# Storing the last 26 rows of a spectrum as cells of both parts, and regrouping the rows of the product that reads them

## The chip, the cores and the metric

The kernel runs on one core of one Trainium2 chip. TensorE (PE) multiplies matrices and writes to the PSUM banks, VectorE (DVE), ScalarE (ACT) and GpSimd (POOL) work on PSUM or SBUF, and SyncE (SP) issues nearly all DMAs, which 16 DMA engines carry out. The metric is the time of one execution on the device in microseconds. Three runs of the kernel before gave 803.3, 807.4 and 810.25 us, median 807.4 us. The profile is of one more execution, which took 805.76 us; the span from its first to its last instruction is 803.7 us.

## The reference

```python
def _attn_ref(x, h):                      # x (8, 5696, 128), h (5696, 128)
    B, S, D = x.shape
    L = 2 * S
    Yf = np.fft.rfft(x, n=L, axis=1) * np.fft.rfft(h, n=L, axis=0)[None]
    return np.fft.irfft(Yf, n=L, axis=1)[:, :S, :]

def _moe_ref(x, phi, w1, w2):             # x (45568, 128), phi (128, 32), 8 experts, F = 1024
    logits = x @ phi
    d = softmax(logits, over all 45568 tokens)
    slot_input = (d.T @ x).reshape(8, 4, 128)
    slot_out = relu(slot_input[e] @ w1[e]) @ w2[e]     # per expert e, 32 slots in all
    return softmax(logits, over the 32 slots) @ slot_out
```

A long causal convolution of eight sequences with one filter per channel is followed by a soft mixture of experts on the 45568 tokens that come out. Everything is float32.

## The kernel before

The convolution is a two-step Fourier transform of size 90 x 64 written as matrix products. Stage A (`low`, `high`, `fold`; lines 208 to 252) multiplies the input with the table `s1`. Stage B does, for each of 90 frequencies k (64 "main" ones and 26 more), a small transform forward (`stage_b1`, line 287), the product with the filter's spectrum on DVE (lines 306 and 313), and a small transform backward (`stage_b2`, line 328, result `bz`, copied by ACT into `zst`, line 333). Between the stages the data is turned round through DRAM: `fst` goes out to `fl` and `fh` and comes back as `gt`, and `zst` goes out to `zm` (the 64 main frequencies) and `zr` (the other 26) and comes back as `zc` and `zx`. In the last batches further buffers `zd` and `zy` are used.

Stage C works on 32 tiles of tokens, T = 0 to 31, four for each of the eight sequences. `stage_c1` (called `product` in the written order) is the last product of the transform. For each T it makes four PSUM banks `ps[o, c]`, with o for the cosine or sine half of z and c for its real or imaginary part. Each bank is [128, 512]: the upper and the lower 64 partitions hold two fold halves h_ = 0 and 1, of which 45 rows each carry results, and the 512 columns are 4 rows n of 128 channels. The main product (line 419) sums over 64 frequencies: the rows of SBUF are (o, k), so a matmul uses 64 rows and 64 columns of the PE array. The product that this change is about (line 424) adds the other 26 frequencies: the rows of `zx` are (o, c, k), 32 for each of the four pairs (o, c), of which 26 are used. Eight matmuls of 26 rows by 64 columns do it, one for each pair (o, c) and each half h_: rows by (o, c), columns by h_.

After the product ACT copies `ps[0, 1]` (line 427, tile `y`) and `ps[1, 0]` (line 428, tile `om`) to SBUF, and DVE forms sums and differences with `ps[0, 0]` and `ps[1, 1]` (lines 411 and 412). `sums` finishes them on POOL, in the tail of the kernel partly on DVE (line 437). Then come transposes (line 447), logits (456), exponentials, and the dispatch product (546). After all tiles come the experts (lines 801 to 836) and the output product (883).

All instructions are recorded in an order that is written out by hand: the strings of words in the calls of `run` (lines 648 to 725 and 842 to 853). Each word calls one stage for one tile, each engine executes its share in that order, and semaphores order the engines among each other. DMAs of results are collected in `pending` and issued by SP at the word `flush`; loads are issued where `loadf`, `loadx`, `loadz`, `loadr` or `load` stand. The pool of PSUM banks for stages A and C has four members until line 726 and eight afterwards.

The store of the last 26 rows is in `stage_b2`, lines 348 to 352: for each half o two DMAs, one for the real and one for the imaginary part, each reading 64 partitions and moving runs of 128 numbers (512 bytes). The load is `load_rest`, line 392: runs of 4 KB for each partition, 8 KB where two tiles come at once. The row order in z is set by `back` (line 54), a permutation of the columns of the backward table `vt`.

Of the kernel before, what the change touches and what calls it, by code (L numbers as in the profile page):

```python
# [12 lines left out]
F32 = mybir.dt.float32  # L13
# [6 lines left out]
def transform_tables(S, N1, N2, CH, LOW, MAIN):  # L20

    N, R1, HALF, P = N1 * N2, S // N2, N2 // 2, 2 * N2  # L30
    k1 = np.arange(N1)
    alpha = np.pi * (k1 + 0.5) / N1
    m1 = np.arange(R1) - (N1 - 1) / 2
    a1 = np.outer(m1, alpha)
    part = np.stack([np.cos(a1), -np.sin(a1), -np.cos(a1)], 1)
    s1 = np.zeros((P, 3, N2 + HALF))
    for p, r in ((slice(0, P, 2), slice(0, N2)), (slice(P - 4 * (R1 - N2) + 1, P, 4), slice(N2, R1))):
        s1[p, :, 0:LOW] = part[r, :, 0:LOW]
        s1[p, :, N2:N2 + N1 - LOW] = part[r, :, LOW:]
    a0 = np.outer(alpha, np.arange(N1 // 2) + 0.5)  # L40
    part = np.stack([np.cos(a0), -np.sin(a0), -np.cos(a0)], 1)
    NP = N1 // 2
    im = np.zeros((2, MAIN, 2, N2))
    ir = np.zeros((2, 2, HALF, N2))
    for o in range(2):
        for c in range(2):
            im[o, :, c, 0:NP] = part[0:MAIN, o + c]
            ir[o, c, 0:N1 - MAIN, 0:NP] = part[MAIN:, o + c]
    k2 = np.arange(N2)
    omega = np.pi * (k1[:, None] + 2 * N1 * k2[None] + 0.5) / N  # L50
    m2 = np.arange(HALF) - (N2 - 1) / 2
    a2 = m2[None, :, None] * omega[:, None, :]
    w = np.concatenate([np.cos(a2), np.sin(a2)], 1)
    back = np.arange(N2).reshape(2, HALF).T.reshape(-1)
    NU = (NP + 1) // 2
    turn = (N1 - 1) / 2 * alpha[:, None] + (N2 - 1) / 2 * omega
    wq = np.zeros((2, N2, NP, N2))
    vq = np.zeros((2, N2, NU, 2, N2))
    tn = np.zeros((2, N2, 2, (NU + 1) // 2, 2, 2))
    rows = np.arange(N2).reshape(2, HALF // CH, CH)  # L60
    near = rows.reshape(2, -1, 2, CH).transpose(3, 2, 0, 1).reshape(-1)
    far = rows.reshape(2, -1, 2, 2, CH).transpose(4, 2, 3, 0, 1).reshape(-1)
    for a in range(2):
        wq[a] = w[a::2].transpose(1, 0, 2)
        wq[a] = np.concatenate([wq[a][near, 0:LOW // 2], wq[a][far, LOW // 2:]], 1)
        for q in range(NP):
            vq[q % 2, :, q // 2, a] = w[2 * q + a][back].T
            tn[q % 2, :, 0, q // 4, a, q // 2 % 2] = np.cos(turn[2 * q + a]) / N
            tn[q % 2, :, 1, q // 4, a, q // 2 % 2] = np.sin(turn[2 * q + a]) / N
    im, ir, wq, vq, tn = [t.reshape(P, *t.shape[k:]) for t, k in  # L70
                          ((im, 2), (ir, 3), (wq, 2), (vq, 2), (tn, 2))]
    return [np.ascontiguousarray(t, dtype=np.float32) for t in (s1, im, ir, wq, vq, tn)]
# [3 lines left out]
def kernel(  # L76
# [24 lines left out]
    nc = tc.nc  # L101
    P = 128
    B, S, D = x.shape
# [4 lines left out]
    N1, N2 = 90, 64  # L108
    R1, HALF, NP = S // N2, N2 // 2, N1 // 2
# [19 lines left out]
    fh = [nc.dram_tensor(f"fh_{g}", (NJ // 4, 2, CH, 2, 2, 2, HALF // 2, 2 * D), F32, kind="Internal").ap()  # L129
          for g in range(B + 1)]  # L130
    zm = [nc.dram_tensor(f"zm_{b}", (2, MAIN, HALF, 2, D), F32, kind="Internal").ap() for b in range(B)]
    zr = [nc.dram_tensor(f"zr_{b}", (2, 2, HALF, HALF, D), F32, kind="Internal").ap() for b in range(2)]
    cd = nc.dram_tensor("c_t", (P, B * NQ, Q, 2, MH), F32, kind="Internal").ap()

    const = ctx.enter_context(tc.tile_pool(name="const", bufs=1))
# [3 lines left out]
    nc.gpsimd.memset(one[:, :], 1.0)  # L139
    phi = const.tile([D, NSL], F32, name="phi")  # L140
    im = const.tile([P, 2, HP], F32, name="im")
    ir = const.tile([P, HP], F32, name="ir")
    acc = const.tile([P, D + 1], F32, name="acc")
    NT = B * NQ
    TR = HP + MH
# [171 lines left out]
    def stage_b2(u):  # L317
        g, w, us = parts(u)
        if g == 0:
            return  # L320
        m = len(us)
        y_ = prods.pop(u)
        bz = bps.tile([P, 2, 2, 2 * D], F32, name="bz", tag=("bt", "bz")[u % 2])
        for o, (i, n) in enumerate(us):
            for q in range(n):
                r = slice(q * HP, (q + 1) * HP)
                for a in range(2):
                    nc.tensor.matmul(bz[a * HP:(a + 1) * HP, q, o, :], vt[r, i, a, :],  # L328
                                     y_[r, a * m + o, :, :].rearrange("p c d -> p (c d)"),
                                     start=True, stop=True)  # L330
        n = us[0][1]
        e_ = w % 4
        nc.scalar.activation(zst[:, e_, 0:m, 0:n, :].rearrange("p o q x -> p q o x"),  # L333
                             bz[:, 0:n, 0:m, :], AF.Copy)
        if w % 2 == 0:
            return
        k = 4 * e_ + m * n
        sv = zst[:, :, :, :, :].rearrange("p u o q x -> p (u o q) x")
        q0 = 4 * e_ - 4
        k0 = 8 * (w - 1)  # L340
        for o in range(2):
            if k0 < MAIN:
                pending.append(partial(
                    nc.sync.dma_start,
                    out=zm[g - 1][o, k0:k0 + 16].rearrange("(q a) r c d -> (a r) q (c d)", a=2),
                    in_=sv[o::2, q0:k, :]))
                continue
            for c in range(2):
                pending.append(partial(
                    nc.sync.dma_start,  # L350
                    out=zr[g % 2][o, c, k0 - MAIN:k0 - MAIN + 2 * (k - q0)].rearrange("(q a) r d -> (a r) q d", a=2),
                    in_=sv[o::2, q0:k, c * D:(c + 1) * D]))

    zs, ys, Ls, ds = {}, {}, {}, {}
    ybufs = [ypool.tile([P, Q * CH, D + 1], F32, name=f"y{i}") for i in range(2)]
    zring = [ypool.tile([P, 2, CH, 2, D], F32, name="zc")]
    rests, rest = [ypool.tile([P, 2, 2, CH, D], F32, name="zx")], {}
    lt = ypool.tile([P, CH, 2, HP], F32, name="lt")
    dt = ypool.tile([P, CH, 2, HP], F32, name="dt")
    om, op = [ypool.tile([P, CH, D], F32, name=n) for n in ("om", "op")]  # L360
# [8 lines left out]
    def load_main(T):  # L369
        if T >= NT:  # L370
            return
        b, j = divmod(T, NQ)
        t_ = zring.pop(0)
        zring.append(t_)
        zs[T] = t_
        n = 2 * CH
        nc.sync.dma_start(
            out=t_[:, :, :, :, :].rearrange("p h n c d -> p (h n c d)"),
            in_=zm[b].rearrange("o k r c d -> (o k) r (c d)")[:, j * n:(j + 1) * n].rearrange(
                "p r x -> p (r x)"))  # L380

    def load_rest(T):
        if T >= NT:
            return
        b, j = divmod(T, NQ)
        m = 1 if j < 2 else 2
        if j % 2 == 0:
            t_ = rests.pop(0)
            rests.append(t_)
            rest[T] = rest[T + 1] = t_  # L390
        n = 2 * CH
        nc.sync.dma_start(
            out=rest[T][:, j % 2:j % 2 + m, :, :, :].rearrange("p v h n d -> p (v h n d)"),
            in_=zr[(b + 1) % 2].rearrange("o c k r d -> (o c k) r d")[:, j * n:(j + m) * n].rearrange(
                "p r x -> p (r x)"))

    def load_pair(T):
        load_main(T)
# [2 lines left out]
    def stage_c1(T, between=lambda: None):  # L401
# [13 lines left out]
        for c in (1, 0):  # L415
            for h_ in range(2):
                for o in range(2):
                    r = slice(o * HP, (o + 1) * HP)
                    nc.tensor.matmul(ps[o, c][h_ * HP:(h_ + 1) * HP, :], im[r, c, :],  # L419
                                     zt[r, h_, :, c, :], start=True, stop=False)  # L420
        for h_ in range(2):
            for (o, c), p in ps.items():
                r = slice((2 * o + c) * HALF, (2 * o + c) * HALF + N1 - MAIN)
                nc.tensor.matmul(p[h_ * HP:(h_ + 1) * HP, :], ir[r, :], zx[r, h_, :, :],  # L424
                                 start=False, stop=True)
        ps = {k: p[:, :].rearrange("p (n d) -> p n d", d=D) for k, p in ps.items()}
        nc.scalar.activation(part(0, 0), ps[0, 1], AF.Copy)  # L427
        nc.scalar.activation(om[:, :, :], ps[1, 0], AF.Copy)
# [191 lines left out]
    nc.scalar.dma_start(out=phi[:, :], in_=moe_phi)  # L620
    nc.scalar.dma_start(out=turn[:, :, :, :, :], in_=t_turn)
    nc.scalar.dma_start(out=im[:, :, :], in_=t_im)
    nc.scalar.dma_start(out=ir[:, :], in_=t_ir)
    for i in range(8):
        nc.scalar.dma_start(
            out=zr[i // 4][i // 2 % 2, i % 2, N1 - MAIN:].rearrange("k (j r) d -> (k j) (r d)", r=2 * CH),
            in_=rests[0][0:4 * (HALF - N1 + MAIN), 0, :, :, :].rearrange("p h n d -> p (h n d)"))
    held = {}

    def load_w1(e_):  # L630
# [96 lines left out]
    rings.append(mid.enter_context(tc.tile_pool(name="ps2", bufs=4, space=PSUM)))  # L727
    last = work.enter_context(tc.tile_pool(name="last", bufs=1))
    tail["last"] = last
    zring.insert(0, last.tile([P, 2, CH, 2, D], F32, name="zd"))  # L730
    rests.insert(0, last.tile([P, 2, 2, CH, D], F32, name="zy"))
    tail["cT"] = last.tile([P, B, R1, 2 * NJ], F32, name="cT")
    second = inner.enter_context(tc.tile_pool(name="second", bufs=1, side="right"))
    w2s = second.tile([P, E, NFC, D], F32, name="w2s")
# [41 lines left out]
    def expert_in():  # L776
# [14 lines left out]
        nc.vector.tensor_copy(out=own, in_=p[:, 0:NSL].rearrange("p (e s) -> p e s", s=SPE))  # L791
    EG = E // Q
    FH = 512
    hid, hidT = [z_[:, :, :, :, :].rearrange("p h n c d -> p (h n c d)").rearrange(
        "p (g k c) -> p g k c", g=EG, k=NFC) for z_ in zring[::-1]]

    def layer_1(g):
# [138 lines left out]
```

## Time and profile before

| what | value |
|---|---|
| median of three runs (lowest to highest) | 807.4 us (803.3 to 810.25) |
| profiled execution: its time, its span | 805.76 us, 803.7 us |
| PE, DVE, ACT, POOL busy | 712.9, 629.3, 429.3, 410.4 us |
| DMA | 164779 packets, 282.50 MB, mean 352 GB/s |
| main product, line 419 | 512 records of MATMUL (32 tiles x 16) |
| product of the last rows, line 424 | 512 records of MATMUL (32 tiles x 16) |
| stores of `zr` | 32 DMAs of 256 KB and 32 of 160 KB |
| mean granted clock of TensorE | 0.951 |

How to read it: busy times are sums over the whole span, and a matmul's record runs until its modelled end, so overlapping matmuls make PE busy without telling how much it does. Each float32 matmul of the program leaves two MATMUL records and two weight loads: it is done in two passes. The slices and windows tell where in the span an engine is busy, and the chain of work that ended last tells which work set the end.

### The profile page before, as it was taken

The page shows a single profiled execution, that of the slowest core. Times are in us where ns is not written, and L with a number is a line of the kernel's source. Part 1 is how long each engine was busy: PE and PEld are TensorE (multiplying, and loading weights), DVE is VectorE, ACT ScalarE, POOL GpSimd, SP SyncE. Part 2 cuts the span into 40 slices and gives each one's busy share as a digit, 9 for nine tenths or more (in the row PEclk, how much of TensorE's full clock was granted, in tenths as well). Part 3 has the DMA queues.
Part 4 walks back from the last instruction along what each step waited for, and adds up shares of the span by engine and source line. Part 5 has one row for each costly group of instructions (what it writes and reads, how often), then busy time and mean ns, then how long its engine had stood idle before and what let it go on. Part 6 is the DMA issues. An engine that isn't in the chain of part 4 may idle for free.

```text
span 803.7 us, 21826 instructions
## 1 busy us (share of the span) xinstructions
PE 712.9 (89%) x8884; PEld 360.5 (45%) x8884; DVE 629.3 (78%) x895; ACT 429.3 (53%) x868; POOL 410.4 (51%) x368
## 2 busy tenths in 40 slices
PE   5768789779999999999999999999998887888882
PEld 1122233324544444554455455444444444356782
DVE  1019988648989999998999999999989996795552
ACT  2334245335666665666666566666565455474441
POOL 5545443425556666656666655566434533686000
PEclk9889999979999999999999999999999998999865
DMA  8999999999999999999999999999999899843998
GB/s 274 357 308 405 332 391 388 330 361 388 389 351 379 383 388 344 397 393 380 361 394 394 355 386 389 399 355 357 374 309 342 282 363 317 317 179 129 385 401 337
DMA packets 164779, 282.50 MB, mean 352 GB/s; under 512 B 9448, under 2 KB 128872, under 8 KB 158440
## 3 DMA queue, kind: packets, MB, share of 16 engines
q1 hardware_dynamic: 163672, 280.01, 96.1%
q8 instruction: 71, 1.16, 0.5%
q10 hardware_dynamic: 1008, 1.10, 0.4%
q14 instruction: 28, 0.23, 0.1%
HBM read 148.54 MB, written 132.53 MB: 350 GB/s over the span
## 4 chain that ended last, share of the span: by engine, by line
PE 62%; DVE 15%; DMA 14%; ACT 4%; issue 2%; POOL 1%; SPq 1%; ACTq 0%; DVEq 0%; POOLq 0%
PE bank L240 18%; PE bt L287 10%; PE bz L328 8%; PE bank L419 7%; DMA out_dram<-o 4%; PE bank L424 4%; PE bank L447 4%; DMA fl<-fst 4%; DVE yf L306 3%; DVE bt L306 3%; PE bank L456 3%; PE bank L546 2%; DVE yf L313 2%; PE bank L570 2%; DMA gt<-fh 2%
## 5 line engine op out<-in xcount | busy, mean ns | idle before, releaser
L216 POOL TENSOR_TENSOR x<-xc 128x512 f32<-128x512 f32 x144 | 179.1, 1276 | 81.5 <-PE bank L240 53.5
L240 PE MATMUL bank<-x,s 128*32 128x512 f32 x1728 | 207.1, 608 | 14.0 <-POOL x L216 8.1
L242 ACT ACTIVATE fst<-bank 128x512 f32<-128x512 f32 x216 | 125.6, 595 | 84.5 <-PE bank L240 63.3
L287 PE MATMUL bt<-gt,wt 64*64 64x256 f32 x1620 | 117.6, 399 | 26.2 <-DMA gt<-fl 9.7
L333 ACT ACTIVATE zst<-bz 128x1024 f32<-128x1024 f32 x96 | 93.0, 968 | 80.6 <-PE bz L328 74.3
L437 POOL TENSOR_TENSOR y<-y,op 128x512 f32<-128x512 f32 x64 | 78.3, 1223 | 105.2 <-DVE op L411 102.7
L306 DVE TENSOR_TENSOR yf<-bt,Hi 128x1024 f32<-128x1024 f32 x96 | 112.4, 1171 | 16.2 <-PE bt L287 16.1
L313 DVE TENSOR_TENSOR yf<-bt,yf 128x512 f32<-128x512 f32 x192 | 119.3, 663 | 3.3
L306 DVE TENSOR_TENSOR bt<-bt,Hr 128x1024 f32<-128x1024 f32 x96 | 113.0, 1177 | 0.0
L240 PEld LDWEIGHTS bank<-x,s 128*32 128x32 f32 x1728 | 52.2, 111 | 131.8 <-issue 91.8
L328 PE MATMUL bz<-yf,vt 64*64 64x256 f32 x1440 | 100.6, 387 | 4.6 <-DVE yf L313 4.2
L287 PEld LDWEIGHTS bt<-gt,wt 64*64 64x64 f32 x1620 | 54.9, 135 | 87.9 <-issue 35.6
L533 POOL TENSOR_TENSOR L<-L,rs 128x512 f32<-128x512 f32 x32 | 33.6, 1051 | 109.3 <-DVE rs L528 89.5
L328 PEld LDWEIGHTS bz<-yf,vt 64*64 64x64 f32 x1440 | 55.7, 136 | 39.8 <-DVE yf L313 11.8
L437 POOL TENSOR_TENSOR y<-y,om 128x512 f32<-128x512 f32 x54 | 64.1, 1187 | 2.1
L427 ACT ACTIVATE y<-bank 128x512 f32<-128x512 f32 x32 | 19.1, 597 | 81.6 <-PE bank L424 81.6
L447 PE MATMUL bank<-ident,y 109*128 109x109 f32 x512 | 59.4, 261 | 3.1 <-DVE y L437 1.0
L419 PE MATMUL bank<-zc,im 64*64 64x512 f32 x480 | 60.3, 600 | 0.0
L447 PEld LDWEIGHTS bank<-ident,y 109*128 109x128 f32 x512 | 49.7, 141 | 12.7 <-issue 7.9
L306 DVE TENSOR_TENSOR yf<-bt,turn 128x1024 f32<-128x1024 f32 (+1 forms) x12 | 14.0, 1170 | 52.4 <-PE bt L287 52.4
L449 ACT ACTIVATE yt<-bank 128x360 f32<-128x360 f32 x128 | 52.6, 475 | 3.7 <-PE bank L447 3.5
L883 PE MATMUL op<-so,cT 32*128 32x128 f32 x704 | 43.6, 357 | 6.5 <-ACT o L891 6.0
(99 smaller groups left out, 854.9 us busy)
## 6 DMA issues: line engine op xcount, KB each, us to landing
fl<-fst SPq DMA_DIRECT2D x72, 512.0 KB, 7.7
gt<-fl SPq DMA_DIRECT2D x72, 512.0 KB, 7.2
zm<-zst SPq DMA_DIRECT2D x64, 512.0 KB, 9.3
zc<-zm SPq DMA_DIRECT2D x30, 1024.0 KB, 9.1
fh<-fst SPq DMA_DIRECT2D x36, 512.0 KB, 6.6
xc<-in_x_dram SPq DMA_DIRECT2D x32, 512.0 KB, 8.8
out_dram<-o SPq DMA_DIRECT2D x16, 1024.0 KB, 11.2
gt<-fh SPq DMA_DIRECT2D x27, 512.0 KB, 8.2
```

The lines of the kernel that those rows point to most:

```text
L216: nc.gpsimd.tensor_tensor(out=y_[:, o, :, :], in0=near, in1=far, op=AL.subtract if o else AL.add)
L240: nc.tensor.matmul(p[i * m:(i + 1) * m, :], s1[:, q + o, cols], columns(c_, o), start=True, stop=True)
L242: nc.scalar.activation(st[:, :, q, :], p[:, :].rearrange("p (n d) -> p n d", d=D), AF.Copy)
L287: nc.tensor.matmul(bt[q * HP:(q + 1) * HP, a, o, :], wt[r, 2 * i + q, :], t_[r, 2 * o + q, :, :].rearrange("p c d -> p (c d)"), start=True ...
L306: nc.vector.tensor_tensor(out=p_, in0=pv, in1=h_, op=AL.mult)
L313: nc.vector.tensor_tensor(out=y_[r, 0:k, c, :], in0=pv[:, :, c, :], in1=y_[r, 0:k, c, :], op=op_)
L328: nc.tensor.matmul(bz[a * HP:(a + 1) * HP, q, o, :], vt[r, i, a, :], y_[r, a * m + o, :, :].rearrange("p c d -> p (c d)"), start=True, sto ...
L333: nc.scalar.activation(zst[:, e_, 0:m, 0:n, :].rearrange("p o q x -> p q o x"), bz[:, 0:n, 0:m, :], AF.Copy)
L419: nc.tensor.matmul(ps[o, c][h_ * HP:(h_ + 1) * HP, :], im[r, c, :], zt[r, h_, :, c, :], start=True, stop=False)
L437: eng.tensor_tensor(out=part_, in0=part(v, 0), in1=o_[:, :, :], op=sign)
L447: nc.tensor.transpose(p[:, i * TR:(i + 1) * TR], ys[T][0:TR, k * CH + i, 0:D], ident[0:TR, 0:TR])
L449: nc.scalar.activation(yt[:, k * CH:(k + 1) * CH, :, :], of_tokens(p), AF.Copy)
```

## The change

The last rows of z are stored as cells that hold both parts, real and imaginary, one behind the other. `zr` becomes (o, h, k, m, c, d): the fold half h moves to the outside, the part c to the inside. A store reads 32 partitions (every fourth) and moves runs of 256 numbers (1 KB); there are still four stores for each group of frequencies. The rows of `zx` are then (o, h, k), and its columns (m, c, d). So the matmuls of the last rows are grouped by (o, h) on the row side: the pair (o, h) picks both the rows and the column half, and the part c picks a slice of the moving data and a table in `ir`. They are issued by part, first for the banks `ps[0, 1]` and `ps[1, 0]`, then for the other two. Their stationary operand has 45 columns in place of 64, since the 19 zero columns are gone. For both products to see the same rows, the order of the backward columns (`back`) changes, and with it the layout of `zc`: (n, h, c, d) in place of (h, n, c, d). The written order of the stages is the same.

```diff
-    ir = np.zeros((2, 2, HALF, N2))
+    ir = np.zeros((2, 2, HALF, 2, NP))
...
-            ir[o, c, 0:N1 - MAIN, 0:NP] = part[MAIN:, o + c]
+            ir[o, :, 0:N1 - MAIN, c] = part[MAIN:, o + c]
...
-    back = np.arange(N2).reshape(2, HALF).T.reshape(-1)
+    back = np.arange(N2).reshape(2, -1, 2, CH).transpose(1, 3, 2, 0).reshape(-1)
...
-    zr = [nc.dram_tensor(f"zr_{b}", (2, 2, HALF, HALF, D), F32, kind="Internal").ap() for b in range(2)]
+    zr = [nc.dram_tensor(f"zr_{b}", (2, 2, HALF, HALF // 2, 2, D), F32, kind="Internal").ap() for b in range(2)]
...
-    ir = const.tile([P, HP], F32, name="ir")
+    ir = const.tile([P, 2, MH], F32, name="ir")
...
-            for c in range(2):
+            for h_ in range(2):
                 pending.append(partial(
                     nc.sync.dma_start,
-                    out=zr[g % 2][o, c, k0 - MAIN:k0 - MAIN + 2 * (k - q0)].rearrange("(q a) r d -> (a r) q d", a=2),
-                    in_=sv[o::2, q0:k, c * D:(c + 1) * D]))
+                    out=zr[g % 2][o, h_, k0 - MAIN:k0 - MAIN + 2 * (k - q0)].rearrange(
+                        "(q a) m c d -> (a m) q (c d)", a=2),
+                    in_=sv[2 * h_ + o::4, q0:k, :]))
...
-    zring = [ypool.tile([P, 2, CH, 2, D], F32, name="zc")]
-    rests, rest = [ypool.tile([P, 2, 2, CH, D], F32, name="zx")], {}
+    zring = [ypool.tile([P, CH, 2, 2, D], F32, name="zc")]
+    rests, rest = [ypool.tile([P, 2, CH, 2, D], F32, name="zx")], {}
...
-            in_=zr[(b + 1) % 2].rearrange("o c k r d -> (o c k) r d")[:, j * n:(j + m) * n].rearrange(
-                "p r x -> p (r x)"))
+            in_=zr[(b + 1) % 2].rearrange("o h k m c d -> (o h k) (m c d)")[
+                :, j * CH * 2 * D:(j + m) * CH * 2 * D])
...
-                                     zt[r, h_, :, c, :], start=True, stop=False)
-        for h_ in range(2):
-            for (o, c), p in ps.items():
-                r = slice((2 * o + c) * HALF, (2 * o + c) * HALF + N1 - MAIN)
-                nc.tensor.matmul(p[h_ * HP:(h_ + 1) * HP, :], ir[r, :], zx[r, h_, :, :],
-                                 start=False, stop=True)
+                                     zt[r, :, h_, c, :], start=True, stop=False)
+        for c in (1, 0):
+            for o in range(2):
+                for h_ in range(2):
+                    r = slice((2 * o + h_) * HALF, (2 * o + h_) * HALF + N1 - MAIN)
+                    nc.tensor.matmul(ps[o, c ^ o][h_ * HP:h_ * HP + MH, :], ir[r, c ^ o, :],
+                                     zx[r, :, c ^ o, :], start=False, stop=True)
```

More of the change, by code (lines that the diff above doesn't have):

```diff
@@ L377, in load_main @@
         nc.sync.dma_start(
-            out=t_[:, :, :, :, :].rearrange("p h n c d -> p (h n c d)"),
+            out=t_[:, :, :, :, :].rearrange("p n h c d -> p (n h c d)"),
             in_=zm[b].rearrange("o k r c d -> (o k) r (c d)")[:, j * n:(j + 1) * n].rearrange(
@@ L390, in load_rest @@
             rest[T] = rest[T + 1] = t_
-        n = 2 * CH
         nc.sync.dma_start(
-            out=rest[T][:, j % 2:j % 2 + m, :, :, :].rearrange("p v h n d -> p (v h n d)"),
-            in_=zr[(b + 1) % 2].rearrange("o c k r d -> (o c k) r d")[:, j * n:(j + m) * n].rearrange(
-                "p r x -> p (r x)"))
+            out=rest[T][:, j % 2:j % 2 + m, :, :, :].rearrange("p v n c d -> p (v n c d)"),
+            in_=zr[(b + 1) % 2].rearrange("o h k m c d -> (o h k) (m c d)")[
+                :, j * CH * 2 * D:(j + m) * CH * 2 * D])
     def load_pair(T):
@@ L622 @@
     nc.scalar.dma_start(out=im[:, :, :], in_=t_im)
-    nc.scalar.dma_start(out=ir[:, :], in_=t_ir)
+    nc.scalar.dma_start(out=ir[:, :, :], in_=t_ir)
     for i in range(8):
         nc.scalar.dma_start(
-            out=zr[i // 4][i // 2 % 2, i % 2, N1 - MAIN:].rearrange("k (j r) d -> (k j) (r d)", r=2 * CH),
-            in_=rests[0][0:4 * (HALF - N1 + MAIN), 0, :, :, :].rearrange("p h n d -> p (h n d)"))
+            out=zr[i // 4][i // 2 % 2, i % 2, N1 - MAIN:].rearrange(
+                "k (j m) c d -> (k j) (m c d)", m=CH),
+            in_=rests[0][0:4 * (HALF - N1 + MAIN), 0, :, :, :].rearrange("p n c d -> p (n c d)"))
     held = {}
@@ L729 @@
     tail["last"] = last
-    zring.insert(0, last.tile([P, 2, CH, 2, D], F32, name="zd"))
-    rests.insert(0, last.tile([P, 2, 2, CH, D], F32, name="zy"))
+    zring.insert(0, last.tile([P, CH, 2, 2, D], F32, name="zd"))
+    rests.insert(0, last.tile([P, 2, CH, 2, D], F32, name="zy"))
     tail["cT"] = last.tile([P, B, R1, 2 * NJ], F32, name="cT")
@@ L793 @@
     FH = 512
-    hid, hidT = [z_[:, :, :, :, :].rearrange("p h n c d -> p (h n c d)").rearrange(
+    hid, hidT = [z_[:, :, :, :, :].rearrange("p n h c d -> p (n h c d)").rearrange(
         "p (g k c) -> p g k c", g=EG, k=NFC) for z_ in zring[::-1]]
```

## The prediction

> **What bounds the kernel now.** I began with the chain of work that ended last (part 4 of the page). PE holds 62% of it, and line 424, the product that the change regroups, stands on it with 4.0%, about 32 us. Its 32 tiles at 1.04 us, a duration read below, make 33.3 us, so nearly all of it sets the end.
>
> ```profile
> PE 62%; DVE 15%; DMA 14%; ACT 4%; issue 2%; POOL 1%; SPq 1%; ACTq 0%; DVEq 0%; POOLq 0%
> ```
>
> Then the busy times by stretch: from 188 to 564 us PE is busy for 375.62 of 376.00 us at a granted clock of 1.00, and the list of PE's waits in that stretch is empty.
>
> ```profile
> core 0: us, PE busy (x) PEld busy (x) DVE busy (x) ACT busy (x) POOL busy (x), PEclk, DMA share, GB/s
> 188.00:564.00 376.00, 375.62 (x4788) 185.82 (x4788) 345.56 (x482) 239.08 (x480) 233.54 (x199) 1.00 1.04 378
> ```
>
> A busy PE need not be a full one, so I looked at one tile in the same chain, restricted to 243 to 247 us (columns: start, us, what):
>
> ```profile
> 243.90 1.88 PE bank L419 x16
> 245.78 1.04 PE bank L424 x16
> 246.82 1.02 PE bt L287 x16
> ```
>
> Both products have 16 records over the same 512 columns, yet the main one takes 1.88 us and the last rows take 1.04 us. The timeline, asked for stretches of 50 ns, tells why (start, us, what; four answers, the first two from line 419):
>
> ```profile
> 244.31 0.61 PE L419 MATMUL bank<-zc,im 64*64 64x512 f32 x4
> ...
> 244.74 0.61 PE L419 MATMUL bank<-zc,im 64*64 64x512 f32 x4
> ...
> 245.71 0.68 PE L424 MATMUL bank<-zx,ir 26*64 26x512 f32 x8
> ...
> 246.19 0.63 PE L424 MATMUL bank<-zx,ir 26*64 26x512 f32 x8
> ```
>
> PE works in waves. Line 419 has four matmuls at a time, in the four quarters of 64 rows by 64 columns; its waves start at 243.83, 244.31, 244.74 and 245.17, so a following wave takes 0.43 us. Line 424 has eight at a time, one for each pair of 32 rows (four groups) and 64 columns (two halves), and is through in two waves: 245.71 to 246.19 (0.48), and 246.19 to 246.75 (0.56, with the change to the next shape).
>
> **The change part by part.** The order of all instructions on each engine is as before; only shapes, addresses and the order inside the last product differ.
>
> *The product of the last rows.* Before, rows go by (o, c) and columns by h_, so eight matmuls occupy eight different places of the array. After, the row group is (o, h) and the column half is h: the half picks both. Only four places are left, (group 0, left), (1, right), (2, left), (3, right), each used by two matmuls, c = 1 and c = 0. The other four stand idle. Sixteen passes over four places are four waves, as in line 419. Two more waves at 0.43 us are 0.86 us: 0.48 + 0.43 + 0.43 + 0.56 = 1.90 us in place of 1.04. The bounds: below, 0, if something other than places makes the waves; above, a doubled wave (a rival). I take 0.86, since line 419 has the same sixteen passes on four places. Forty-five columns in place of 64 change no place (45 is more than 32) and no wave, which is set by the 512 moving columns. The weight loads go from 64 to 45 columns; they lie under the wave before (0.23 us of load in 1.04).
>
> *Where the 0.86 us counts.* Products 1 to 20 (190 to 545 us) lie in the stretch where PE waits for nothing: 20 x 0.86 = 17.2 us. Nothing hides it there: DVE, next fullest, has 345.56 of 376 us.
>
> Product 0 (171.5 us) is on the chain with PE behind it: 0.86 us. Ahead of it stand a store of `zr` (7.23 us) and the load of `zx` (5.06 us); a faster store may give back 0.4. Together 0.5 us.
>
> Products 21 to 31 (564 to 709 us) lie where PE is no longer full, and the chain leaves them through ACT and DVE:
>
> ```profile
> 616.73 1.12 PE bank L424 x16
> 617.85 0.59 ACT y L427
> 618.46 0.70 DVE y L411
> ```
>
> ACT needs only `ps[0, 1]`, which is complete after the c = 1 matmuls: two of the four waves, 0.91 us against 1.04, so it starts some 0.1 us sooner and ends about 1.6 us after the product's start. DVE also needs `ps[0, 0]`, complete after 1.90 us and a drain of 0.07: it starts at about 1.97 where it started at 1.71. The step costs 0.26 us. The chain has five such products (564, 617, 669, 685, 698): 1.3 us. The product at 600 has PE behind it: 0.86. The one at 580 goes through ACT's copy `om`, with `bz` on PE behind the product: between 0 and 0.86, taken 0.5. Three (630, 649, 691) are off the chain, hidden by DVE or a DMA, and may come onto it: 0.3 each, 0.9. The last (708) is hidden by reductions on DVE up to 710.66 us, 0.3. Together 3.9 us.
>
> *The stores.* In the trace's DMA records a packet of 512 bytes takes 27.7 ns in the mean (26752 of them, nearly all stores of `zr`), one of 1024 bytes 46.6 ns. Over 16 engines 26752 x 27.7 / 16 = 46.3 us become 13376 x 46.6 / 16 = 38.9 us: 7.3 us less DMA time in the whole span, 0.9 for each of eight batches. In the full stretch it is worth nothing, because PE waits for no DMA there. In the tail a store of `zm` (7.18 us) and a load (12.33 us) are on the chain from 636 to 657 us, while two batches' stores go out between 575 and 670: half of 1.8, 0.9 us gained. Bounds: 0 and 7.3. SP issues as many stores as before; a store of either size needs at least 0.58 us to issue, so I count no change. Sixteen engines still get equal shares, two partitions each instead of four. The loads of `zx` and the filling of its zero rows move the same runs of 4 and 8 KB.
>
> *Layouts.* The main product's moving data steps by 2 KB instead of 1 KB, and the last rows' by 1 KB instead of lying together. Line 419 (stepped) and 424 (not stepped) have nearly the same record, 589 and 587 ns, so a step costs nothing here: 0, bounded by those 2 ns for each wave. `ir` is loaded once at the start, 360 bytes for each partition in place of 256: under 0.1 us. The columns of `vt` are only permuted: 0. No wait is added on any engine.
>
> *The sum.* 17.2 + 0.5 + 3.9 - 0.9 = 20.7 us. From the profiled execution's own 805.76 us this gives 826.5. The median of the runs lies 1.6 us higher, so 827 to 828; I say 827. A difference under about 1% can't be told from none in this kernel, whose three runs already spread by 0.9%.
>
> **The rivals.**
>
> *Two row groups in one bank.* Before, a bank is always filled by one row group: `ps[o, c]` by group (o, c) in line 424, by half o in line 419. After, `ps[0, 1]` is written at once by row group 0 (partitions 0 to 44) and row group 1 (64 to 108). If a bank takes one row group at a time, waves of four become waves of two: four more at 0.43 us, 1.7 us more for each product. Twenty products in the full stretch cost 34 us more, the rest about 8, and the time is 869. Against it: the writes go to different partitions, and lines 287 and 328 have two matmuls writing one bank at once without losing a wave, though from one row group. No row of this trace shows two groups in one bank; 7%.
>
> The Trainium skill, TensorEngine Tiling (Array Packing), section Restrictions and Gotchas, says that different row tiles cannot access the same PSUM bank simultaneously. By that rule it would be this rival; the trace of before neither shows nor contradicts it.
>
> *Not slower: the waves don't lengthen.* If the 0.43 us of a wave were set by the 64 rows of line 419, and 26-row passes for one place followed each other without waiting, the last product would stay at 1.04 us. Then only the stores count: 0.4 at product 0, 0.9 to 1.8 in the tail, with ACT's start 0.1 us sooner six times: 2 to 3 us, 803 us. It decides at the place: second passes must start before 0.43 us are over. Against it, the second wave of line 424 starts 0.48 us after the first although its rows are few; and the 7.3 us of DMA time can't be got where PE waits for none. 10%.
>
> *Slower, but partly given back.* DMA queues run with a share of 1.04 beside the full PE. A slower PE asks for less per microsecond, and the tail's wait of 12.33 us for `gt` could shrink by some 5 us, with the off-chain products staying off: 805.8 + 17.2 + 0.5 + 2.5 - 6 = 820, and 814 with a few hidden products. 12%, half of it under 818.
>
> **How the numbers follow.** Forecast (0.86 us per product, 818 to 838): 68%. Given back: 12%. Not slower: 10%. One bank, one group: 7%. Something dearer in between, such as a drain between waves of the new shape (838 to 850): 3%. The range for 8 in 10 is 816 to 839: it takes in the forecast and most of the given-back case; the unknown ends of stores and tail (7.3 us less, 4 us more) lie within it. Faster by over 1%: 2%, the not-slower case with nearly all of the stores' 7.3 us and more. Within 1% (to 815.5 us): 11%, the rest of that case and the low end of the given-back one. Slower by over 1%: 87%.
>
> **What would show it.** In the changed kernel's timeline the last product (line 425) should have four matmuls at a time, in waves 0.43 us apart, and take 1.9 us; the full stretch should still have no wait of PE, and its four-product period should go from 74.8 us to about 78.2. Packets under 2 KB should fall by 13376. Eight at a time, or 1.04 us, would refute the forecast; waves of two would make it the bank. If the product takes 1.9 us but the period doesn't grow by 3.4 us, PE wasn't the bound.

## The result

The changed kernel is slower: 826.2 us (median of six runs, 821.87 to 829.44) against 805.8 us for the kernel before (median of six, 803.3 to 810.25), a ratio of 1.0247 with a 95% interval from 1.0207 to 1.0288. 827 us had been forecast. A second measurement of the same kernel, beside other runs, gave 824.9 us and a ratio of 1.0223 (1.0183 to 1.0264). The profiled execution took 829.44 us, of which the span is 827.3.

The busy times of the changed kernel for the full stretch (188 to 580 us, the columns as in the prediction) show that PE still waits for hardly anything, at a granted clock of 1.00:

```profile
188.00:580.00 392.00, 390.81 (x4772) 190.57 (x4772) 344.68 (x481) 239.21 (x478) 230.17 (x196) 1.00 1.00 361
```

The chain of work, restricted to 267 to 275 us, has the last two products as neighbours again (start, us, what; the product of the last rows is now line 425):

```profile
269.65 1.88 PE bank L419 x16
271.52 1.86 PE bank L425 x16
273.38 1.02 PE bt L287 x16
```

1.86 us stand where 1.04 stood. The timeline of the changed kernel, asked at four moments inside this product, has four matmuls at each:

```profile
271.45 0.64 PE L425 MATMUL bank<-zx,ir 26*45 26x512 f32 x4
...
271.92 0.61 PE L425 MATMUL bank<-zx,ir 26*45 26x512 f32 x4
...
272.35 0.61 PE L425 MATMUL bank<-zx,ir 26*45 26x512 f32 x4
...
272.78 0.61 PE L425 MATMUL bank<-zx,ir 26*45 26x512 f32 x4
```

The reader sees four waves, 0.43 to 0.47 us apart, where there were two waves of eight. The share of line 425 in the whole chain rises from 4.0% to 7.5%:

```profile
PE 65%; DVE 12%; DMA 11%; ACT 4%; POOL 3%; issue 2%; SPq 2%; ACTq 0%; DVEq 0%; POOLq 0%
```

The stores did what they were meant to do. In the list of DMA issues their median time to landing falls from 5.2 to 4.3 us (256 KB) and from 3.8 to 3.4 us (160 KB), and the packets from 164779 to 151466:

```profile
zr<-zst SPq DMA_DIRECT2D x32, 256.0 KB, 4.3
...
zr<-zst SPq DMA_DIRECT2D x32, 160.0 KB, 3.4
```

To see where the time went, I set the starts of the products of the last rows, from the traces' records, against each other (us):

| | before | changed | changed, second trace |
|---|---|---|---|
| start of product 0 | 171.5 | 173.4 | 170.9 |
| from product 0 to 1 | 18.9 | 20.2 | 19.2 |
| from product 1 to 20 | 354.5 | 371.0 | 371.0 |
| from product 20 to 31 | 163.5 | 167.6 | 166.1 |
| from product 31 to the end of the span | 95.4 | 95.1 | 95.3 |

The stretch from product 1 to 20 takes 16.5 us more in both traces of the changed kernel; it is most of the loss. By the records 15.5 us of it are the nineteen products themselves (35.34 us from the start of each to PE's next matmul, summed, against 19.85).

### The profile page after: what moved, and what is told of

The parts are those of the page before. It is cut to its first block, busy times and chain, and to the rows that moved or that the text cites. A ratio compares the mean times of both kernels' runs of the same rounds, so it can differ in the third digit from the quotient of the medians.

```text
span 827.3 us, 21837 instructions
## 1 busy us (share of the span) xinstructions
PE 738.8 (89%) x8884; PEld 367.8 (44%) x8884; DVE 630.1 (76%) x895; ACT 431.1 (52%) x868; POOL 410.5 (50%) x368
## 2 busy tenths in 40 slices
DMA packets 151466, 282.50 MB, mean 341 GB/s; under 512 B 9448, under 2 KB 115560, under 8 KB 145128
## 3 DMA queue, kind: packets, MB, share of 16 engines
q10 hardware_dynamic: 1008, 1.11, 0.4%
## 4 chain that ended last, share of the span: by engine, by line
PE 65%; DVE 12%; DMA 11%; ACT 4%; POOL 3%; issue 2%; SPq 2%; ACTq 0%; DVEq 0%; POOLq 0%
PE bank L240 18%; PE bt L287 9%; PE bz L328 8%; PE bank L425 7%; PE bank L419 7%; PE bank L448 4%; DMA out_dram<-o 4%; DVE yf L306 3%; PE bank L457 3%; DVE bt L306 3%; PE bank L547 2%; PE op L885 2%; DVE yf L313 2%; DMA fl<-fst 2%; POOL y L438 2%
## 5 line engine op out<-in xcount | busy, mean ns | idle before, releaser
L287 PE MATMUL bt<-gt,wt 64*64 64x256 f32 x1620 | 115.7, 394 | 27.1 <-DMA gt<-fl 10.1
L328 PE MATMUL bz<-yf,vt 64*64 64x256 f32 x1440 | 98.9, 382 | 4.2 <-DVE yf L313 3.9
L425 PE MATMUL bank<-zx,ir 26*45 26x512 f32 x480 | 59.6, 611 | 7.6 <-DMA zx<-zr 7.5
L411 DVE TENSOR_TENSOR y<-bank,y 128x512 f32<-128x512 f32 x32 | 22.1, 690 | 43.5 <-PE bank L425 41.3
```

The costliest lines, as they stand in the source:

```text
L287: nc.tensor.matmul(bt[q * HP:(q + 1) * HP, a, o, :], wt[r, 2 * i + q, :], t_[r, 2 * o + q, :, :].rearrange("p c d -> p (c d)"), start=True ...
L425: nc.tensor.matmul(ps[o, c ^ o][h_ * HP:h_ * HP + MH, :], ir[r, c ^ o, :], zx[r, :, c ^ o, :], start=False, stop=True)
```

## The experiments

My theory was that the places of the PE array which the eight matmuls use make the whole difference. The rivals were the new stores, the new layouts with their longer steps, and the two row groups that write one bank at once.

**Four places in the kernel before.** One line of the kernel before sends the matmuls to the half c in place of h_; the bookkeeping of the accumulation groups follows it. Stores, layouts and row groups stay.

```diff
+        four = True
...
-                                     zt[r, h_, :, c, :], start=True, stop=False)
+                                     zt[r, h_, :, c, :], start=True,
+                                     stop=four and h_ != c)
...
-                nc.tensor.matmul(p[h_ * HP:(h_ + 1) * HP, :], ir[r, :], zx[r, h_, :, :],
-                                 start=False, stop=True)
+                half = c if four else h_
+                nc.tensor.matmul(p[half * HP:(half + 1) * HP, :], ir[r, :], zx[r, h_, :, :],
+                                 start=False, stop=not four or h_ == 1)
```

> The kernel before, with stores, loads, layouts and row groups unchanged; only the eight matmuls of the last rows go to the column half c in place of h_, so that they use four places of the array in place of eight (the wrong rows are added up; the work is otherwise the same). If the places make the cost: four waves, about 1.9 us a product, the stretch 20 x 0.86 = 17.2 us longer, and the tail dearer than in the changed kernel, since here all four banks are complete only after the fourth wave: 824 to 834 us. If the cost lay in the stores, the cell layout, the stepped reads or two row groups writing one bank, none of which is here: 803 to 809 us.

Measured: 831.0 us, ratio 1.0321 (1.0277 to 1.0364), inside the expected span and far from 803 to 809. The chain of this kernel:

```profile
251.91 1.88 PE bank L420 x16
253.78 1.88 PE bank L427 x16
```

The last product (line 427 here) takes 1.88 us, as long as the main one (420). With nothing of the change but the number of places, the whole loss is there, and some more (here all four banks are complete only after the fourth wave).

**Eight places in the changed kernel.** The reverse: everything of the change stays, but the matmuls of c = 0 go to the other half.

```diff
-                    nc.tensor.matmul(ps[o, c ^ o][h_ * HP:h_ * HP + MH, :], ir[r, c ^ o, :],
+                    half = h_ if c else 1 - h_
+                    nc.tensor.matmul(ps[o, c ^ o][half * HP:half * HP + MH, :], ir[r, c ^ o, :],
```

> The changed kernel with everything kept, but the matmuls of c = 0 go to the other column half, so that eight places are in use again (the halves of two banks are swapped, so the result is another one; the work is the same). If the places make the whole cost: two waves, about 1.04 us a product, 802 to 806 us, that is the time before or up to 3 us less for the stores. If something else of the change costs (layouts, stores from 32 partitions), it stays above 809 us by that part. If the stores of 1 KB were worth their 7.3 us of DMA time, it would be near 798 us.

Measured: 804.4 us, ratio 0.9985 (0.9964 to 1.0007). The chain:

```profile
262.28 1.88 PE bank L419 x16
264.15 1.03 PE bank L426 x16
```

The loss is gone, and the stores with their 7.3 us less DMA time (the prediction's estimate) are worth between 2.9 us and nothing. This is a net amount: the trace takes 357.2 us from product 1 to 20, 2.7 more than that of the kernel before, and 159.5 us from 20 to 31, 4.0 less (1.1 less than the layouts alone, below). These two runs settle the main question from both sides.

**The layouts alone.** The kernel before with the new order of rows, so that moving data is read with longer steps; `zr` keeps cells of 512 bytes.

```diff
-                                     zt[r, h_, :, c, :], start=True, stop=False)
+                                     zt[r, :, h_, c, :], start=True, stop=False)
...
-                nc.tensor.matmul(p[h_ * HP:(h_ + 1) * HP, :], ir[r, :], zx[r, h_, :, :],
+                nc.tensor.matmul(p[h_ * HP:(h_ + 1) * HP, :], ir[r, :], zx[r, :, h_, :],
```

> The kernel before with the new order of the backward columns and the new order (n, h, c, d) and (n, h, d) inside the loaded tiles, so that moving data is read with the longer steps; zr keeps its 512-byte cells, the row groups and eight places are those of before. My theory: no change, ratio 0.997 to 1.003, records of lines 419 and 424 at 587 to 589 ns. If longer steps in the moving data cost anything, the two products lengthen and the time rises by 20 us for each us.

Measured: 805.5 us, ratio 1.0003 (0.9983 to 1.0022); the two products take 1.88 and 1.04 us as before. A cost of the steps can't be seen.

**The order in which the places are asked for.** Two runs keep the change and only issue its eight matmuls in another order. The first goes by half o:

```diff
-        for c in (1, 0):
-            for o in range(2):
+        for o in range(2):
+            for c in (1, 0):
                 for h_ in range(2):
```

> The changed kernel with the eight matmuls issued by half o first: row groups 0 and 1 with c = 1, the same two places with c = 0, then groups 2 and 3. If a place that is busy holds only its own matmuls back and those behind it may pass: still four waves of four, 1.86 us, and the time of the changed kernel, 822 to 830 us, though ACT gets its second bank later. If a matmul that waits for its place holds everything behind it: waves of two, at least 2.7 us a product, 17 us more or above: 843 us and more.

Measured: 824.3 us, ratio 1.0233 (1.0202 to 1.0264), four waves, 1.87 us a product: not to be told from the changed kernel. The second puts the two matmuls of a place directly behind each other:

```diff
-        for c in (1, 0):
-            for o in range(2):
-                for h_ in range(2):
+        for o in range(2):
+            for h_ in range(2):
+                for c in (1, 0):
```

> The changed kernel with the two matmuls of each place issued directly one after the other (group 0 c = 1, group 0 c = 0, group 1 c = 1, and so on). If a matmul may pass one that waits for its place: four waves of four as before, 1.86 us, 822 to 830 us. If four waiting passes for one place are more than can be passed: at most two places at work, 2.7 us or more a product, 843 us and above.

Measured: 833.7 us, ratio 1.0317 (1.0283 to 1.0351). Neither case was met. The product takes 1.88 us in four waves of four, so matmuls do pass others that wait for their place. The records bear this out: in one product of the full stretch (number 10) the four matmuls of the first wave start at 0, 6, 13 and 20 ns in the changed kernel, at 0, 7, 27 and 34 ns with the halves first, and at 0, 13, 27 and 40 ns with the pairs together, that is with a gap wherever the written order has matmuls that must wait. Yet the kernel is some 9 us slower than the changed one measured beside it (824.9). The waits of both kernels show what differs. Of the changed kernel:

```profile
ACT y L428 <- PE bank L425: 82.7, 31, 12.0
...
DVE y L411 <- PE bank L425: 41.3, 27, 13.4
```

and of the one with the pairs together:

```profile
ACT y L428 <- PE bank L425: 105.5, 32, 9.6
...
DVE y L411 <- ACT y L428: 56.4, 30, 11.2
```

ACT waits 23 us longer for the product. By the records it starts its first copy 1.96 us after the product's start, in place of 1.11, in nearly every tile, that is after the fourth wave and not after the second, and DVE starts 2.59 us after it in place of 2.03. Whether the passes of c = 1 really end later in this order, or are only reported later because a matmul issued ahead of them is still running, the records can't tell, since they don't name the part. Shown is that the order of issue doesn't change the waves but decides when a bank is handed on. With the halves first, too, the second bank, whose matmuls stand behind two of c = 0, reaches ACT 2.02 us after the start in place of 1.60. All three orders fit a bank that is handed on only when everything issued ahead of it is through; no run tests this by itself.

The late hand-over is not the whole of the 9 us. Against the second trace of the changed kernel this one takes 1.1 us more from product 0 to 1 (20.3), 3.8 more from 1 to 20 (374.8), and 3.8 more from 20 to 31 (169.9). The four-place kernel, whose banks are also all complete only at the end, has the same 1.96 us; from 20 to 31 it takes 170.5 us, but from 1 to 20 only 370.2. So the late hand-over fits the tail. In the stretch the pairs-together kernel has a wait of PE that neither the four-place nor the changed kernel has there (188 to 564 us):

```profile
PE bank L240 <- DVE y L412: 3.3, 5, 0.7
```

PE waits for a bank five times, once every four products. Why it does so in this kernel alone stays open.

**Where the cost falls.** Two runs use four places in the kernel before for some tiles only (the same edit as in the first experiment, with `four = 1 <= T <= 20` and `four = T > 20`).

> The kernel before with four places for the last rows only in products 1 to 20, those of the stretch where PE waits for nothing; the other twelve keep eight. If each of them is paid in full: 20 x 0.82 to 0.86 = 16.4 to 17.2 us over the kernel before of the same call, 821 to 823 us. If the tail gives part back (a lighter DMA load, hidden products), less: 812 to 818 us.

Measured: 820.3 us, ratio 1.0160 (1.0124 to 1.0195), that is 10.0 to 15.7 us, less than the 16.4 expected at least. The trace is nearer: from product 1 to 20 it takes 370.3 us in place of 354.5, 15.8 more than the kernel before for 19 products, 0.83 each, so in the stretch each is paid in full. The missing part isn't explained by one row: from product 20 to 31 this trace takes 161.1 us, where the kernel before took 163.5, but the layout kernel, with the same products, 160.6.

> The kernel before with four places only in products 21 to 31. The four-place kernel was 26 us slower in all; less 17 for the stretch and 0.9 for product 0 leaves some 8 us for these eleven, 0.75 us each: 811 to 815 us. This is more than the 3.9 us of the prediction, since here ACT too waits for the fourth wave. If the tail hid its products behind DVE and DMA, it would be under 808 us.

Measured: 814.4 us, ratio 1.0105 (1.0074 to 1.0137), 8.5 us for eleven products, as expected. Its trace takes 170.6 us from product 20 to 31, against 163.5 and 160.6 for the kernel before and the layout kernel. So the tail does not hide them when ACT, too, has to wait for the fourth wave. The two ratios together give 2.65%, the kernel with all four-place products has 3.21%; product 0 (below) is 0.2 of what is missing, the rest lies within the intervals.

**The changed kernel once more.**

> The changed kernel once more, to see what of its first trace repeats: the product in 1.86 us and the period of four products in 78.2 us should return; product 0, which began 2.3 us later than in the kernel before, should begin anywhere from 170 to 174 us if that was the spread of the start, and near 173.7 us again if the change delays it.

Measured: 824.9 us; product in 1.86 us, 371.0 us from product 1 to 20. Product 0 began at 170.9 us, earlier than in the kernel before, so the late start of the first trace was spread: over all ten traces it begins between 170.1 and 175.1 us. In the five with stores of 1 KB the mean is 171.1, in the five others 173.0; the first trace of the changed kernel has 173.4, so this is a hint of what the stores give back, no proof.

## Why the prediction was right, and where its steps were off

*Waves and places* held. Forecast were four waves and 1.90 us; measured 1.86, since by the records the first wave takes 0.46 and the last 0.54 us where 0.48 and 0.56 were carried over from the kernel before. That the number of places is the cause, argued beforehand from line 419 alone, is shown by the first two experiments in both directions.

*The full stretch* held: forecast 17.2 us for 20 products, measured 16.5 from product 1 to 20, which holds 19 of them. The period of four products, forecast at 78.2 us, is 78.2 and 78.4 (311.0 to 389.2 and 232.7 to 311.0 us). Nothing was given back there, so that rival falls for the stretch. The same stretch is not the same in every trace, though: with eight places it takes 354.5 (kernel before), 354.5 (layouts), 356.2 (tail only) and 357.2 us (eight places of the change); with four, 370.2 to 371.2, and 374.8 with the pairs together.

*No wait is added on any engine*, says the prediction, and this step looks off by about 1 us. In the full stretch the changed kernel has five semaphore instructions of PE at line 457 (51 ns each), one in each group of four products. The other runs with 1 KB stores have them, too, at the same place; the kernel before and the runs built on it have none. What they wait for, work of DVE at line 552, had ended 0.04 us before each of them began. In all five traces with them the matmuls of line 328, which stand just ahead, take 53.0 us from product 1 to 20 up to PE's next work; in the five without, 52.0 or 52.1. That is most of what the 16.5 us hold beyond the products themselves. That the instructions cause it is not shown by a run of its own.

*Product 0* was mis-sized. I took 0.86 us for its two more waves; they cost 1.65 us: the product takes 3.59 us against 1.94 (3.04 in the second trace, 1.1 more). The granted clock was overlooked. The stretch of the kernel before around this product has

```profile
171.40:173.40 2.00, 1.94 (x16) 0.33 (x17) 0.00 (x0) 0.00 (x0) 0.00 (x0) 0.50 1.00 320
```

and the changed kernel

```profile
173.40:177.00 3.60, 3.56 (x16) 0.67 (x16) 0.00 (x0) 1.09 (x2) 0.00 (x0) 0.50 1.01 350
```

The clock (third column from the right) is 0.50 after PE had waited 5.8 us (before) and 7.5 us (changed) for the load, and a wave takes 0.85 to 0.91 us there. The trace of before showed that. In the second trace of the changed kernel PE had waited 3.6 us; the first wave still took 0.46 us, the second 0.69, and 0.85 came only with the third (granted clock 0.82 from 170.9 to 171.9 us, 0.50 from there to 174.1).

*The tail* held in its mechanism. ACT was to start 0.1 us sooner and DVE 0.26 us later; by the records of the full stretch and of most tail products ACT starts 1.11 us after the product's start against 1.17, DVE 2.03 against 1.80. A chain piece of the changed kernel shows DVE following the product directly, where ACT's copy stood between them before:

```profile
621.51 1.93 PE bank L425 x16
...
623.48 0.70 DVE y L411
```

The size can't be told closely: from product 20 to 31 the two traces of the changed kernel average 166.9 us, those of the kernel before and of the layout kernel 162.0. The 4.8 us between them hold product 20, 0.8, so 4.0 are left against a forecast of 3.9 less 0.9 for the stores; the traces of one kind differ by up to 2.9. Against the eight-place run with the same stores (159.5) the products alone would be 6.5 us, and the stores would give back 2.5: both terms look too small, and their errors go against each other, but each rests on one or two traces.

*The stores* were right in size as DMA time (13376 packets fewer were forecast, the page of the profile has 13313 fewer), and worth little on the path: forecast 1.3 us, measured 0 to 2.9.

*The bank rival* falls. In a wave of the changed kernel row groups 0 and 1 fill `ps[0, 1]` together, at partitions 0 to 44 and 64 to 108, and a wave takes the same 0.43 us. The Trainium skill, TensorEngine Tiling (Array Packing), section Restrictions and Gotchas, says different row tiles cannot access the same PSUM bank simultaneously. This case's runs do not agree where the two write different partitions: four at a time in the lines above, and no lost wave. Two row tiles on the same partitions of one bank were not tried.

*Not slower* falls with the waves: passes of 26 rows take the same 0.43 us a wave as passes of 64.

*The total* came out closer than its terms: 827 us forecast, 826.2 and 824.9 measured. This is in part luck. The prediction adds 20.7 us; the two measurements are 20.4 and 17.9 us above the medians of the kernel before that they were taken with, the spans of the two traces of the changed kernel differ by 4.8 us, and product 0, the semaphore instructions and the tail were each off by 0.2 to 2.6 us.

## What to carry to other kernels

Count the different places (row group by column half) that a group of small matmuls occupies, not the matmuls: regrouping data for the sake of DMA is dear when row group and column half then depend on the same index, because half of the array stands idle. Before saving on transfers, look for the stretch where they would have to count: in the full stretch PE waited for none of them, so 13 thousand packets fewer bought at most 3 us, while 0.82 us more for each product was paid there in full. And within a group, issue first, and directly behind each other, the matmuls that fill the bank which the next engine needs first: with the pairs together, one matmul of another bank between the two went along with the late hand-over.

## What the runs showed of the hardware

Matmuls that wait for a busy place did not hold back those behind them: whatever the order of issue, even with four passes for one place in a row, four places were kept at work in waves of 0.43 us. The order still moved the release of the first bank from 1.11 to 1.96 us after the start. The kernel with that order was about 9 us slower than the changed one: 3.8 us of it fell in the tail, as in the four-place kernel with the same 1.96 us, 3.8 in the full stretch, where that kernel loses nothing by it.

Two row groups filled one PSUM bank at the same time, on different partitions, without a lost wave (0.43 us).
